# Interleaving the last block's first two accumulations, and moving two of the previous block's stores from SyncE to GpSimd

## The chip, the cores and the metric

The kernel runs on one core of one Trainium2 chip. The metric is the device time of one execution in microseconds, taken as the median of several runs. The kernel before the change has a median of 667.27 us over three runs (666.69 to 668.64). Beside these runs there is one profiled execution with its own time.

## The reference

The input `x` has 8 sequences of 4096 tokens with 192 channels, in float32. The computation has two stages.

```python
# stage 1: causal convolution of 7 taps per channel; 8 heads of 24 channels share their taps
w = exp(weight - max) / (sum + 1e-9)                 # weight: 8 x 7, a softmax over the taps
out[b, s, h, g] = sum_k w[h, k] * x_pad[b, s + k, h, g]   # 6 zero tokens ahead of each sequence
# stage 2: a feed-forward layer over all 32768 tokens
h = x @ w_in                                          # 192 -> 2048
g = 0.5 * h * (1.0 + erf(h / sqrt(2)))                # exact GELU
return g @ w_out                                      # 2048 -> 192, float32
```

## The kernel before

The 32768 tokens are cut into two halves of 16384, and each half into 35 blocks: six of 256 tokens and then 29 of 512 (`WS`, line 33). A block always takes its tokens from both halves at once. The blocks are numbered 0 to 34, so block 34 is the last (`NB - 1`) and block 33 the one ahead of it (`NB - 2`).

For one block the work runs through the engines like this. SyncE (SP) issues the loads of `x`. VectorE (DVE) transposes them and, with some first taps done by ScalarE (ACT), computes the convolution into `xc`. TensorE (PE) multiplies by `w_in` into two PSUM buffers `hp` (line 1292). ACT applies GELU and writes `gT` (line 1199). PE multiplies `gT` by `w_out` into the four PSUM banks `ob`. DVE or ACT copies the result to the buffer `osb` in SBUF (there are two, used in turn), and DMAs store it to the output in HBM.

The second product comes in several forms. Block 33 is one of the blocks (`ST`, line 75) whose second product is built from sums of `gT` blocks, so that fewer products are needed (line 1426). Its four banks must then be combined. ACT copies parts out (`st_copy`, line 782). GpSimd (POOL) issues two small DMAs, `cg` and `cu`, that move 64 partitions to the other 64 (`st_dma`, line 686). DVE adds them (lines 803 and 797) and writes three transposed pieces into `osb` (line 815); these pieces are the events `ev` of the list for stage 35 (line 109). The last of them, `ev.1.33`, ends block 33.

Block 33 is then stored by `store` (line 829): one wait for `S_EV`, followed by four DMAs, `q` = 0 to 3. Each has 32 partitions with 16 runs of 96 floats, which is 512 runs of 384 bytes or 192 KB. Before the change SP issues all four (line 845).

Block 34 has no other block behind it to share PE with. Its second product (line 1482) is done in four groups `g` of 128 tokens. Each group has two accumulations `h`, one for each half of the tokens, each into a PSUM bank of its own and with 16 products (`NF` = 16), one for each 128 rows of `w_out`. Before a group starts, `wait_banks` (line 416) waits until both of its banks are free: groups 0 and 2 use the `ob` banks that block 33 leaves, groups 1 and 3 the `hp` buffers. In group 0, with `h` = 0, every fourth product also waits for the GELU that it needs; the 13th waits for the last GELU of the kernel. When an accumulation is complete it is copied out, for `h` = 0 by DVE (line 449) and for `h` = 1 by ACT (line 451). Each is then stored by one DMA of 96 KB (`store_half`, line 459), issued by SP for `h` = 0 and by ACT itself for `h` = 1.

Nothing reorders this. Each engine works through a list in the order in which the code writes it, and waits for semaphores: `S_GELU`, `S_MM2` (an accumulation is done), `S_EV` (DVE has written a piece), `S_OUT` (a store has landed; one for each `osb` buffer). At the end SP waits until both `S_OUT` counts are full (line 1516). Then all five engines meet at the end of the block of code (the trace gives this line 201): each runs a DRAIN, the other four announce themselves to POOL, and POOL, after its own DRAIN, releases all.

POOL's own list ends with `cg` and `cu` of block 33 (`GLIST`, line 858), so its DRAIN comes right behind these two DMAs.

Of the kernel before, what the change touches and what calls it, by code (L numbers as in the profile page):

```python
# [11 lines left out]
def bass_lightweight_conv__then__act_gelu_exact_kernel(  # L12
# [10 lines left out]
    F2, C = moe_w_out.shape  # L23
# [13 lines left out]
    NB = len(WS)  # L37
# [3 lines left out]
    NF = F // 128  # L41
# [27 lines left out]
    SL0 = [sum(NSL[:n]) for n in range(NB + 1)]  # L69
    NG = [w // 128 for w in WS]  # L70
# [111 lines left out]
    OUTS = []  # L182
# [12 lines left out]
    def sem(name):  # L195
        return es.enter_context(nc.semaphore(name))
# [4 lines left out]
    with es:  # L201
# [37 lines left out]
        S_XIN = [sem("S_XIN%d" % i) for i in range(NX)]  # L239
        S_XP = sem("S_XP")  # L240
        S_OUT = [sem("S_OUT%d" % i) for i in range(2)]
        S_MSET = sem("S_MSET")
        S_WNM = sem("S_WNM")
        S_IDN = sem("S_IDN")
# [581 lines left out]
                    ap(xin[n % NX], 32 * q * (TB // 32 * DQ), dst), ap(xt, off, src)  # L826
                ).then_inc(sm or S_XIN[n % NX], 16)

        def store(e, m):
            if m < M0:  # L830
                for g in range(NG[m]):
                    wait_ev(e, m, g)
                    e.dma_start(
                        ap(
                            outt,
                            (OFF[m] + 128 * g) * C,
                            [[C, 128], [HALF * C, 2], [1, C]],
                        ),
                        ap(osb[m % 2], g * C, [[8 * C, 128], [4 * C, 2], [1, C]]),
                    ).then_inc(S_OUT[m % 2], 16)  # L840
                return
            wait_ev(e, m, NP - 1)
            for q in range(4):

                e.dma_start(
                    ap(
                        outt,
                        ((q // 2) * HALF + OFF[m]) * C + (q % 2) * (C // 2),
                        [[C, 32], [32 * C, WS[m] // 32], [1, C // 2]],
                    ),  # L850
                    ap(
                        osb[m % 2],
                        32 * q * 8 * C,
                        [[8 * C, 32], [C // 2, WS[m] // 32], [1, C // 2]],
                    ),
                ).then_inc(S_OUT[m % 2], 16)

        GLIST = (
# [15 lines left out]
        @block.gpsimd  # L874
        def _(g):
            def win_in(q, hf, sm):
                c0, pat = part(q)
                g.dma_start(  # L878
                    ap(win, 64 * hf * NP * F + c0, pat), ap(wint, c0 + FQ * hf, pat)
                ).then_inc(sm, 16)  # L880

            g.wait_ge(S_MSET, 1)
            for hf in range(2):
                m = idb[64 * hf : 64 * hf + 64, :]
                g.affine_select(
                    out=m,
                    in_=m,
                    compare_op=ALU.is_equal,
                    fill=0.0,
                    base=0,  # L890
                    pattern=[[-1, 64]],
                    channel_multiplier=1,
                ).then_inc(S_IDN)
            g.wait_ge(S_IDN, 2)
            g.memset(wnm[:, :], 0.0).then_inc(S_WNM)
            g.memset(ap(xTb[0], HF, [[NP * XB, 128], [XB, NP], [1, HB]]), 0.0).then_inc(S_HALO)
            for q in range(2):
                for hf in range(2):
                    win_in(q, hf, S_WIN[(hf, 2 + 3 * hf)[q]])
            g.wait_ge(S_PRO, 9)  # L900
            g.tensor_tensor(  # L901
                ap(dg, 3 * 64, [[KS * 64, 128], [64, KS - 3], [1, 64]]),
                ap(idb, 0, [[64, 128], [0, KS - 3], [1, 64]]),
                ap(wcol, 3, [[32, 128], [1, KS - 3], [0, 64]]),
                ALU.mult,
            ).then_inc(S_DG)

            def wout_in(k):
                g0, gs = ((0, 1), (4, 1), (2, 4), (3, 4))[k]
                g.dma_start(  # L910
                    ap(wout, 2 * g0 * C, [[NF * C, 128], [2 * gs * C, 2], [1, 2 * C]]),
                    ap(woutt, 256 * g0 * C, [[2 * C, 128], [256 * gs * C, 2], [1, 2 * C]]),
                ).then_inc(S_WOUT[k], 16)

            def halo(n):

                t, tw = (xTb[PC[n]], XB) if n in PC else (xT[n % 2], XW)
                dst = ap(t, HF, [[NP * tw, 128], [tw, NP], [1, HB]])
                if n >= 4:
                    g.wait_ge(S_CV, cvd(n - 2))  # L920
                if OFF[n] % SEQ == 0:
                    g.memset(dst, 0.0).then_inc(S_HALO)
                    return
                g.wait_ge(S_TR, trd(n - 1))
                src = ap(
                    xT[(n - 1) % 2], HF + WS[n - 1], [[NP * XW, 128], [XW, NP], [1, HB]]
                )
                if n == NR:
                    g.wait_ge(S_UH, 1)
                    src = ap(uu, 32 - HB, [[TB, 128], [32, NP], [1, HB]])  # L930
                g.tensor_copy(dst, src).then_inc(S_HALO)

            win_in(2, 0, S_WIN[3])
            load(g, 2, (0,), S_XP)
            halo(1)
            g.wait_ge(S_HALO, 2)
            dup(g, 0, 1)
            win_in(2, 1, S_WIN[4])
            wout_in(0)
            load(g, 2, (2,), S_XP)  # L940
            g.wait_ge(S_DUPP, 1)
            cast(g, 1, 0)
            cast(g, 1, 1)
            load(g, 2, (1,), S_XP)
            wout_in(1)
            cast(g, 1, 2)
            load(g, 2, (3,), S_XP)
            wout_in(2)
            wout_in(3)
            halo(2)  # L950
            def win_again(k):
                g.wait_ge(S_MM1, SL0[NR - 1] + (4, 8, 14, 16)[k])
                c0 = 2 * FQ * (0, 2, 1, 3)[k]
                for hf in range(2):
                    for p in range(NP):
                        g.dma_start(
                            ap(win, (64 * hf * NP + p) * F + c0, [[NP * F, 64], [1, 2 * FQ]]),
                            ap(wint, RUN * p * F + c0, [[GRP * F, 8], [F, RUN], [1, 2 * FQ]]),
                        ).then_inc(S_WR[k], 16)

            for n in range(3, 10):
                halo(n)
                for k in {NR: (0,), NR + 1: (1, 2, 3)}.get(n, ()):
                    win_again(k)
            for op in GLIST.split():
                name, *q = op.split(".")
                if name == "halo":
                    halo(int(q[0]))
                else:
                    st_dma(g, int(q[1]), name, int(q[0]))  # L970

        @block.vector
        def _(v):
# [238 lines left out]
        def _(t):  # L1212
# [261 lines left out]
            m = NB - 1  # L1474
            for g in range(NG[m]):
                wait_banks(t, m, g)
                for h in range(2):
                    for i in range(NF):
                        if (g, h) == (0, 0) and i % 4 == 0:
                            t.wait_ge(S_GELU, SL0[m] + i + 4)  # L1480
                        c0 = (2 * i * NG[m] + 2 * g + h) * 128
                        ins = t.matmul(  # L1482
                            banks(m, g)[h],
                            gT[m % 2][:, c0 : c0 + 128],
                            wout[:, CH[h][i] * C : (CH[h][i] + 1) * C],
                            start=(i == 0),
                            stop=(i == NF - 1),
                        )
                    ins.then_inc(S_MM2)

        @block.sync
        def _(sp):
            sp.dma_start(wsb[:, :], ap(wt, 0, [[KS, H], [1, KS]])).then_inc(S_WSB, 16)
            load(sp, 0, (0, 1))

            sp.wait_ge(S_PRO, 2)
            load(sp, 1)
            sp.wait_ge(S_WOUT[3], 16)
            load(sp, 3)
            load(sp, 4)  # L1500
            xs = 5
            for n in range(1, NB):
                while xs < min(NB, AHEAD.get(n, n + 5)):
                    load(sp, xs)
                    xs += 1
                if n + 4 == NR:
                    for q in range(4):
                        sp.dma_start(
                            ap(p5s, 32 * q * TB, [[TB, 32], [1, DQ]]),
                            ap(xt, (q // 2 * HALF + OFF[n + 4] - 32) * D + DQ * (q % 2), [[D, 32], [1, DQ]]),  # L1510
                        ).then_inc(S_XH, 16)
                store(sp, n - 1)
            for g in range(NG[NB - 1]):
                store_half(sp, g, 0)
            for s in range(2):
                sp.wait_ge(S_OUT[s], OUTS[NB - 1 if (NB - 1) % 2 == s else NB - 2])


# [26 lines left out]
```

## Time and profile before

| | us |
|---|---|
| median of three runs | 667.27 |
| time of the profiled execution | 665.89 |
| its span, first to last instruction | 664.2 |
| PE busy | 658.3 (99%) |
| DVE busy | 619.1 (93%) |
| ACT busy | 598.3 (90%) |
| POOL busy | 106.7 (16%) |
| granted TensorE clock | 1.000 |
| time from the end of the last store's issue (ACT, 662.12) to the end of the span | 2.0 |

All times inside the execution count from its first instruction. The change touches only the last 15 us, so the table is of little use by itself: what matters is a timeline of the stretch from 649 to 664 us, engine by engine, and the times at which DMAs are issued and land. A row of the timeline has start, duration, engine, line, operation, the tiles, how many instructions it stands for, and in square brackets how long the engine sat idle ahead of it and what released it. An engine's name with a q behind it (SPq, ACTq, POOLq) is its sequencer, which issues DMAs, waits and drains.

### The profile page before, as it was taken

Reading aid. Unit: us, or ns where it says so; the run is one execution under the profiler, and the core shown is the slowest. Engines: PE = TensorE matmul, PEld = TensorE weight load, DVE = VectorE, ACT = ScalarE, POOL = GpSimd, SP = SyncE. Lnnn points to the kernel's source line nnn. Section 1 sums busy time; section 2 is a strip of 40 time slices with the busy share of each in tenths; the row PEclk is TensorE's granted clock in tenths of the full one; section 3 lists DMA queues with packets and bytes.
Section 4 is the critical chain, followed back from the end, with each engine's and each line's share of the span. In section 5 each row is a group of like instructions: output and inputs, shape, how many; then the busy total and the mean of one; then the engine's idle time right before and its main releaser. Section 6 shows DMA issues by size and latency. Waiting matters only on the chain.

```text
span 664.2 us, 27974 instructions
## 1 busy us (share of the span) xinstructions
PE 658.3 (99%) x12792; PEld 505.6 (76%) x12792; DVE 619.1 (93%) x555; ACT 598.3 (90%) x707; POOL 106.7 (16%) x175
## 2 busy tenths in 40 slices
PE   8999999999999999999999999999999999999998
PEld 8999655576778988777878755767777888777887
DVE  6999879999999999999999999999999999999962
ACT  8899999898899899999989998988998988899883
POOL 7000430102010110202120102011212020111110
PEclk9999999999999999999999999999999999999999
DMA  9749493935673691677444348947545855352364
GB/s 156 163 95 181 74 156 82 218 64 116 150 146 80 141 206 25 164 168 150 94 116 114 65 106 207 200 108 168 113 106 120 177 117 126 66 113 49 86 142 112
DMA packets 146438, 83.66 MB, mean 126 GB/s; under 512 B 129936, under 2 KB 138192, under 8 KB 146320
## 3 DMA queue, kind: packets, MB, share of 16 engines
q1 hardware_dynamic: 129328, 49.42, 34.8%
q0 software_dynamic: 15872, 31.86, 23.7%
q8 instruction: 100, 1.64, 1.1%
q10 hardware_dynamic: 1120, 0.59, 0.3%
q14 instruction: 18, 0.15, 0.1%
HBM read 31.51 MB, written 25.17 MB: 85 GB/s over the span
## 4 chain that ended last, share of the span: by engine, by line
PE 96%; DMA 2%; ACT 1%; DVE 0%; issue 0%; POOL 0%; ACTq 0%; DVEq 0%
PE hp L1292 49%; PE ob L1426 25%; PE ob L1377 16%; PE ob L1332 5%; DMA win<-in_moe_w_in_dram 1%; PE hp L1482 1%; PE ob L1482 1%; DMA p5s<-u 1%; ACT gT L1199 0%; DMA wsb<-in_weight_dram 0%; DVE wcol L996 0%; POOL win L381 0%; DVE p5s L803 0%; POOL win L878 0%; POOL dg L901 0%
## 5 line engine op out<-in xcount | busy, mean ns | idle before, releaser
L1199 ACT ACTIVATE gT<-hp 128x1024 bf16<-128x1024 f32 x510 | 513.3, 1022 | 52.4 <-PE hp L1292 44.8
L1292 PE MATMUL hp<-xc,win 64*64 64x512 bf16 (+2 forms) x6036 | 438.6, 366 | 0.6 <-DVE win L381 0.5
L1292 PEld LDWEIGHTS hp<-xc,win 64*64 64x64 bf16 (+1 forms) x6036 | 241.8, 105 | 75.9 <-ACT gT L1199 7.3
L359 DVE SCALAR_TENSOR_TENSOR acc<-xT,wcol,acc 128x1536 f32<-128x1536 f32 (+1 forms) x165 | 282.0, 1709 | 8.3 <-ACT acc L1157 5.4
L1426 PE MATMUL ob<-gT,wot 64*64 64x512 bf16 x1152 | 219.1, 376 | 0.0
L1426 PE MATMUL ob<-gT,wst 64*64 64x512 bf16 (+2 forms) x1152 | 203.4, 323 | 0.5 <-DVE p5s L803 0.5
L1377 PE MATMUL ob<-gT,wot 64*64 64x512 bf16 x1920 | 135.8, 376 | 0.0
L1426 PE MATMUL ob<-s_S,wot 64*64 64x512 bf16 (+2 forms) x864 | 132.7, 305 | 0.0
L1426 PEld LDWEIGHTS ob<-gT,wst 64*64 64x64 bf16 x1152 | 98.8, 107 | 15.8 <-DVE p5s L803 1.3
L1377 PEld LDWEIGHTS ob<-gT,wot 64*64 64x64 bf16 x1920 | 71.0, 107 | 32.6
L1426 PEld LDWEIGHTS ob<-gT,wot 64*64 64x64 bf16 x1152 | 88.9, 107 | 8.6
L1426 PE MATMUL ob<-s_S,wst 64*64 64x512 bf16 x288 | 79.5, 376 | 0.0
L1426 PEld LDWEIGHTS ob<-s_S,wot 64*64 64x64 bf16 x864 | 68.8, 107 | 11.0 <-issue 0.3
L1157 ACT ACTIVATE acc<-xT,wcol 128x512 f32<-128x512 f32 (+1 forms) x93 | 64.6, 702 | 0.0
L1023 DVE STREAM_TRANSPOSE xT<-xin 128x1536 f32<-128x1536 f32 (+2 forms) x39 | 59.6, 1536 | 2.9 <-DMA xin<-in_x_dram 1.7
L691 POOL DMA_DIRECT2D gT<-gT x36 | 32.0, 907 | 186.3 <-DVE s_S L734 186.3
L1426 PE MATMUL ob<-s_Dn,wst 64*64 64x512 bf16 x216 | 61.0, 376 | 0.0
L359 DVE SCALAR_TENSOR_TENSOR xc<-xT,wcol,acc 128x1536 bf16<-128x1536 f32 (+1 forms) x33 | 56.5, 1713 | 0.6
L734 DVE TENSOR_TENSOR s_S<-gT 128x1024 bf16<-128x1024 bf16 (+1 forms) x54 | 45.7, 853 | 1.6 <-ACT gT L1199 1.6
L1332 PE MATMUL ob<-wout,gT 64*128 64x192 bf16 x768 | 42.0, 243 | 0.0
L1332 PEld LDWEIGHTS ob<-wout,gT 64*128 64x128 bf16 x768 | 35.1, 94 | 3.3
L1426 PEld LDWEIGHTS ob<-s_S,wst 64*64 64x64 bf16 x288 | 30.8, 107 | 4.4
(100 smaller groups left out, 423.6 us busy)
## 6 DMA issues: line engine op xcount, KB each, us to landing
out_dram<-osb SPq DMA_DIRECT2D x124, 192.0 KB, 3.4
xin<-in_x_dram SPq DMA_DIRECT2D x116, 192.0 KB, 4.5
gT<-gT POOLq DMA_DIRECT2D x18, 512.0 KB, 4.9
gT<-gT POOLq DMA_DIRECT2D x18, 256.0 KB, 4.6
dn<-gT POOLq DMA_DIRECT2D x6, 512.0 KB, 3.0
dn<-s_S POOLq DMA_DIRECT2D x6, 512.0 KB, 6.2
xin<-in_x_dram SPq DMA_DIRECT2D x18, 96.0 KB, 2.4
win<-in_moe_w_in_dram POOLq DMA_DIRECT2D x24, 64.0 KB, 3.3
```

Of the source, the lines that this page charges most:

```text
L359: return e.scalar_tensor_tensor(dst, src, wk, a, op0=ALU.mult, op1=ALU.add)
L691: e.dma_start(quad(m, 1, 0, k, k1 - k), quad(m, 0, 0, k, k1 - k), accum_op=ALU.add).then_inc(S_AD["S3.%d" % q], 16)
L734: ins = v.tensor_tensor(t("S1"), quad(m, 1, 0, k, n), quad(m, 1, 1, k, n), ALU.add)
L1023: v.transpose(out, src).then_inc(S_TR)
L1157: a.activation(out=acc[n % 2][:, p * TB : p * TB + w], in_=ap(xT[n % 2], p * XW + HX, [[NP * XW, 128], [1, w]]), func=AF.Copy, scale=wcol[ ...
L1199: a.activation(out=ap(gT[n % 2], (i % 2 * NF + i // 2) * TB if n in ST else i * c * 2 * w, dst), in_=ap(ob, 2 * TB, [[4 * TB, 128], *src[1 ...
L1292: ins = t.matmul(hbuf(u, slice(fo, fo + fw), o, w), ap(win, f1, [[NP * F, 64], [2, fw]]), xc[n % NXC][r, p * TB : p * TB + w], start=(p == ...
L1332: ins = t.matmul(bb[sub], gT[m % 2][r, c0 : c0 + 128], wout[r, CH[sub][i] * C : (CH[sub][i] + 1) * C], start=(ph == 0 and k == 0), stop=(p ...
L1377: ins = t.matmul(bank(BK[m][j], slice(64 * h, 64 * h + 64), w), ap(wot, 64 * hf * NF * C + CH[h][i] * C + 64 * j, [[NF * C, 64], [1, 64]]) ...
L1426: ins = t.matmul(bank(BK[m][bk], slice(64 * cg, 64 * cg + 64))[:, c0 : c0 + w], wt_, x, start=(e == mine[0]), stop=(e == mine[-1] or e in ...
L1482: ins = t.matmul(banks(m, g)[h], gT[m % 2][:, c0 : c0 + 128], wout[:, CH[h][i] * C : (CH[h][i] + 1) * C], start=(i == 0), stop=(i == NF - 1),)
```

## The change

Two independent edits, both at the end of the kernel.

- Block 34, group 0: instead of 16 products for `h` = 0 and then 16 for `h` = 1, PE does the first 12 of `h` = 0, the first 12 of `h` = 1, then the last four of `h` = 0 and the last four of `h` = 1. The wait for the last GELU stands ahead of the 13th product of `h` = 0 as before, which is now the 25th product of the group. Each accumulation is announced when its last product is done. Groups 1 to 3 are unchanged, and so is the number of products.
- Block 33: SP issues the stores `q` = 0 and 1; POOL issues `q` = 2 and 3, behind its last DMA `cu`, after its own wait for `S_EV`. These two count on a new semaphore `S_OG`, and SP's last waits are changed to match: 32 less on one `S_OUT`, and a further wait for 32 on `S_OG`.

```diff
+        S_OG = sem("S_OG")
...
-        def store(e, m):
+        def store(e, m, parts=range(4)):
...
-            for q in range(4):
+            for q in parts:
...
-                ).then_inc(S_OUT[m % 2], 16)
+                ).then_inc(S_OG if parts[0] else S_OUT[m % 2], 16)
...
                     st_dma(g, int(q[1]), name, int(q[0]))
+            store(g, NB - 2, (2, 3))
...
-                for h in range(2):
-                    for i in range(NF):
-                        if (g, h) == (0, 0) and i % 4 == 0:
-                            t.wait_ge(S_GELU, SL0[m] + i + 4)
...
-                    ins.then_inc(S_MM2)
+                cut = (0, NF - 4, NF) if g == 0 else (0, NF)
+                for i0, i1 in zip(cut, cut[1:]):
+                    for h in range(2):
+                        for i in range(i0, i1):
+                            if (g, h) == (0, 0) and i % 4 == 0:
+                                t.wait_ge(S_GELU, SL0[m] + i + 4)
...
+                        if i1 == NF:
+                            ins.then_inc(S_MM2)
...
-                store(sp, n - 1)
+                store(sp, n - 1, range(4) if n < NB - 1 else (0, 1))
...
-                sp.wait_ge(S_OUT[s], OUTS[NB - 1 if (NB - 1) % 2 == s else NB - 2])
+                sp.wait_ge(S_OUT[s], OUTS[NB - 1] if (NB - 1) % 2 == s else OUTS[NB - 2] - 32)
+            sp.wait_ge(S_OG, 32)
```

More of the change, by code (lines that the diff above doesn't have):

```diff
@@ L1476, in _ @@
                 wait_banks(t, m, g)
-                for h in range(2):
-                    for i in range(NF):
-                        if (g, h) == (0, 0) and i % 4 == 0:
-                            t.wait_ge(S_GELU, SL0[m] + i + 4)
[L1481 to L1488, printed above, removed]
-                    ins.then_inc(S_MM2)
+                cut = (0, NF - 4, NF) if g == 0 else (0, NF)
[4 more added lines that the diff above has]
+                                t.wait_ge(S_GELU, SL0[m] + i + 4)
+                            c0 = (2 * i * NG[m] + 2 * g + h) * 128
+                            ins = t.matmul(
+                                banks(m, g)[h],
+                                gT[m % 2][:, c0 : c0 + 128],
+                                wout[:, CH[h][i] * C : (CH[h][i] + 1) * C],
+                                start=(i == 0),
+                                stop=(i == NF - 1),
+                            )
+                        if i1 == NF:
+                            ins.then_inc(S_MM2)
         @block.sync
```

## The prediction

> **What bounds the kernel now.** I read the chain of waits first, since it says which work ends last, and only then the timeline of the same stretch. The page's shares (PE 99%, DVE 93%) are averages over 35 blocks; the change touches the last 15 us alone.
>
> ```profile
> 649.61 0.46 PE ob L1426 x7
> ...
> 650.58 1.01 ACT gT L1199
> 651.60 0.05 issue
> 651.64 1.82 PE ob L1482 x20
> 653.47 2.64 PE hp L1482 x32
> 656.11 2.64 PE ob L1482 x32
> 658.75 2.65 PE hp L1482 x32
> 661.40 0.02 issue
> 661.42 0.33 ACT osb L451
> ```
>
> Columns: start, length, what. For once the chain leaves PE: at 650 us it goes to the last GELU on ACT, because the 13th product of block 34 waits for it, and returns to PE at 651.64. From there PE runs without a gap to 661.40. The timeline shows what stands beside it:
>
> ```profile
> 649.97 1.16 PE L1482 MATMUL ob<-wout,gT 128*128 128x192 bf16 x12
> ...
> 650.98 0.52 POOL L686 DMA_DIRECT2D p5s<-u  x1 [15.63 <-ACT u L782]
> ...
> 651.64 1.82 PE L1482 MATMUL ob<-wout,gT 128*128 128x192 bf16 x20 [0.51 <-ACT gT L1199]
> ...
> 652.19 0.52 POOL L686 DMA_DIRECT2D u<-u  x1 [0.69 <-issue]
> ...
> 655.73 0.71 DVE L815 STREAM_TRANSPOSE osb<-wtf 128x512 f32<-128x512 f32 x1
> ...
> 656.47 2.60 SPq L845 DMA_DIRECT2D out_dram<-osb  x4
> ...
> 659.12 2.57 SPq L459 DMA_DIRECT2D out_dram<-osb  x4
> ...
> 661.78 0.34 ACTq L459 DMA_DIRECT2D out_dram<-osb  x1
> ```
>
> Block 33 is complete at 656.44 (DVE's last transpose), and SP then issues eight stores without a break until 661.69. The last store of all is ACT's, issued from 661.78; SP's last wait ends at 663.77, 2.0 us later, and the span ends at 664.16. What ends the kernel is thus the last product, its copy, its store; SP's queue is only 0.1 us behind that.
>
> The third view is the one for line 201, where the engines meet at the end. Columns: engine, operation, count, shortest/median/longest in ns, first and last start.
>
> ```profile
> L201 POOLq DRAIN  x1: 7748/7748/7748, 652.2 to 652.2; - x1
> L201 PEldq DRAIN  x1: 1675/1675/1675, 659.8 to 659.8; - x1
> L201 DVEq DRAIN  x1: 397/397/397, 660.1 to 660.1; - x1
> L201 ACTq DRAIN  x1: 153/153/153, 662.2 to 662.2; - x1
> L201 SPq DRAIN  x1: 7/7/7, 663.9 to 663.9; - x1
> ```
>
> All engines must finish theirs. PE's, DVE's and ACT's end within 0.2 us of their engine's last work. POOL's is another thing: it starts behind the last DMA that POOL issues (652.17) and ends at 659.91, though that DMA was issued by 652.71 and had landed by 654.92 (2.73 us after issue). Today this costs nothing: 659.91 lies 4 us ahead of SP's DRAIN at 663.94. The change gives POOL two later DMAs.
>
> **The change, part by part.** The sum is made against the profiled execution (span 664.16, time 665.89, 1.4 us under the median) and its difference is added to the median, 667.27.
>
> *The products of group 0.* 32 products take 2.64 us, so one takes 0.083. Now PE does 12 from 649.97 (to 650.96), stands until 651.64, and does 20 more (to 653.30). After: 24 products from 649.97 last until 651.95, when the GELU is done (651.60), so the wait costs nothing, and the other 8 end at 652.61. That moves PE's end by -0.68, from 661.40 to 660.72. Both banks are already granted ahead of the first product, so no wait is added here. The first accumulation is done some 0.3 us later than now (652.28 against 651.97); hidden, as DVE gets to its copy only after block 33, at 656.37. The next wait is group 2's for banks of block 33: DVE's line 803 frees them at 654.06, and group 2 would start at 655.26. Groups 1 and 3 wait for GELUs that are done. ACT's last store would be issued from 661.10 instead of 661.78 and would end at 663.09.
>
> *Two stores off SP.* SP's four stores took 0.32, 0.49, 0.80 and 0.87 us to issue; the last two go, 1.7 us. SP's half stores of groups 0 to 2 start that much sooner, and the one for group 3 then waits for DVE's copy, which ends at 660.46 now and 659.78 after. SP's end is then no later than ACT's. This does not move more bytes per time: from 657.5 to 662.5 the DMA engines are near full, as the windows show (last two columns: DMA share, GB/s).
>
> ```profile
> 657.50:658.50 1.00, 1.00 (x15) 1.00 (x13) 0.32 (x1) 0.00 (x0) 0.00 (x0) 1.00 0.97 257
> 658.50:659.50 1.00, 1.00 (x15) 1.00 (x14) 0.00 (x0) 0.33 (x1) 0.00 (x0) 1.00 0.88 202
> 659.50:660.50 1.00, 1.00 (x15) 1.00 (x14) 0.36 (x1) 0.00 (x0) 0.00 (x0) 1.00 1.02 271
> ```
>
> The stretch holds about 5.35 us of full DMA work; begun at 657.2 it ends at 662.6, which still allows the end at 663.09 plus 0.4. So without POOL both edits together are worth -0.7, PE's part.
>
> *Two stores on POOL.* They stand behind `cu`, which ends at 652.71, so they wait for nothing but `S_EV`, and start at 656.5. Behind them on POOL there is only the DRAIN, for which all engines wait. No row has 512 runs issued by POOL. Rows: 64 runs 0.52 to 0.59 us (line 686), 256 runs 0.62 to 0.75 (line 825). At 0.15 more for 192 runs, 512 take 0.9. The distance of two issues is uncertain: between the last two it was 1.21, with 0.69 of "issue", at the other pairs about 0.55 (no idle time). I take the gap, as the nearest row at the end of POOL's list: first store 656.5 to 657.4, second 658.1 to 659.0. Without the gap: 657.4 to 658.3.
>
> *The DRAIN.* One row, with three ways to count it. From its start 7.75 us; from the end of the last issue 659.91 - 652.71 = 7.21; from the last landing 659.91 - 654.92 = 4.99. (7.75 would fit a cost for each DMA: POOL issued 128, 60.5 ns each; the trace does not show whether it is so.) After the change these give: from the start, 658.1 + 7.75 = 665.85; from the issue's end, 659.0 + 7.21 = 666.2; from the landing, with 4.1 us from issue to landing as POOL's loads of `x` have, 662.2 + 4.99 = 667.2. I take the middle one. The other DRAINs end behind their engine's last work, and for POOL that is the issue. From the last DRAIN to the end of the span it is 664.16 - 663.94 = 0.22. So the span ends at 666.4, **+2.3**, and the median becomes 669.5. The low end of this case is the start reading without the gap: 657.4 + 7.75 + 0.22 = 665.4, +1.2, 668.5. The high end is the landing reading with the longest landing that SP's stores show near the end, 4.9: 663.0 + 4.99 + 0.22 = 668.2, +4.0, 671.3. In this case PE's 0.7 us are lost: the end no longer hangs on PE.
>
> One rule speaks for a further delay. DVE's copies of line 449 take 1.03 us between 656.37 and 657.82, beside POOL's issues; but POOL issued in 0.56 us at 634.23 and 0.57 at 634.78 with DVE busy throughout, so I add nothing. The Trainium skill's page "SBUF — State Buffer", section "Who interferes with whom", says that certain DVE modes (a float32 copy within SBUF among them) keep GpSimd from writing descriptors; these copies read PSUM. Were it to hold here, it would add up to 1.0.
>
> **The rivals.**
>
> *POOL's DRAIN does not hold the end.* Its length may belong to what POOL did before, not to its last DMAs: there is one row only, and POOL's first DRAIN, before any DMA, took 0.18 us. It decides if the DRAIN lasts under 5.0 us from 658.1, so that it ends before SP's at 663.3. Then the time is 667.27 - 0.7 = 666.6, faster than before, by about 0.1%. Against it: 7.75 us of DRAIN, 5.0 after all had landed, with nothing else on POOL. The Trainium skill's page "VectorE: DVE Perf Modes", section "The DRAIN you can't avoid", says that the DRAINs of preamble and postamble last some 12 ns on all five engines, which would give this rival; SP's 7 ns agree, POOL's 7748 do not, and the row decides.
>
> *The stores by POOL land last.* SP now waits for them too (`S_OG`). They share full DMA engines with SP's and ACT's stores. POOL's landings reach 8.2 us (line 691, accumulating, 4.8 median): 658.1 + 8.2 + 0.4 = 666.7, +2.5, 669.8. It decides from 5.3 us on, as 658.1 + 5.3 = 663.4. For it: full engines. Against: the stretch's work is done at 662.6.
>
> *The change is hidden on PE.* If ACT, SP or the stores ended the kernel without PE, the 0.7 would be zero: 667.3. For it: SP's queue, 0.1 us behind; but that queue gets shorter by 1.7.
>
> **How the numbers follow.** No change can be told from a change of up to 0.3% here, 2.0 us. The DRAIN holds the end: 0.70, of which 0.47 above 669.3 and 0.23 between 668.5 and 669.3. Hidden DRAIN, with PE's gain or without: 0.22, of which 0.17 within 0.3% and 0.05 for faster by more than that, if the stores also clear sooner than I think. Late landing: 0.08, slower. Together: faster 0.05, same 0.40, slower 0.55. The likeliest case gives 669.5. The range reaches down to the hidden DRAIN, 666.6, and 0.1 less, and up to the landing reading, 671.3, so 666.5 to 671.3. The likeliest case's own range is 668.5 to 671.3.
>
> **What would show it.** PE: one unbroken stretch from 649.97 to 660.7. SP: two stores at line 846 instead of four, then half stores from 657.4. POOL: two issues of about 0.9 us between 656.4 and 659.0, and at line 201 a DRAIN that starts near 658 and ends near 666, behind SP's last wait near 663.2. The forecast is wrong if that DRAIN is short, or follows something else than POOL's last issue; and its size is wrong if POOL's issues stand much closer, or if the DRAIN grows with 512 runs.

## The result, and the profile after

The changed kernel took 670.15 us (median of 13 runs, 668.43 to 670.99) against 667.02 us for the kernel before on the same chip (13 runs, 666.23 to 668.64): a ratio of 1.0048, 95% interval 1.0040 to 1.0057. The medians differ by 3.1 us. Its profiled execution took 668.43 us with a span of 666.70 us, 2.5 us longer than the span of before.

The view of the block's closing line, line 201 again, in the kernel after (engine, operation, count, shortest/median/longest in ns, first and last start):

```profile
L201 POOLq DRAIN  x1: 10195/10195/10195, 656.3 to 656.3; - x1
L201 PEldq DRAIN  x1: 1675/1675/1675, 658.2 to 658.2; - x1
L201 DVEq DRAIN  x1: 397/397/397, 658.5 to 658.5; - x1
L201 ACTq DRAIN  x1: 152/152/152, 660.6 to 660.6; - x1
L201 SPq DRAIN  x1: 7/7/7, 663.1 to 663.1; - x1
```

POOL's DRAIN ends at 656.27 + 10.195 = 666.46. Its row starts 0.10 us ahead of the row of POOL's second store (656.37), which the code issues before it, so the start of the row does not say when the DRAIN can begin. SP, which was the last engine before, is done at 663.06 and then stands for 3.4 us. The span ends 0.23 us behind POOL's DRAIN. The four other lines are what they were, to within 1 ns.

The timeline of the last 18 us (start, length, engine, line, operation, out<-in, count, idle time before and what ended it):

```profile
649.04 2.81 PE L1486 MATMUL ob<-wout,gT 128*128 128x192 bf16 x32
...
651.26 0.52 POOL L687 DMA_DIRECT2D u<-u  x1 [0.69 <-issue]
...
654.61 0.71 DVE L816 STREAM_TRANSPOSE osb<-wtf 128x512 f32<-128x512 f32 x1
...
655.35 0.89 SPq L846 DMA_DIRECT2D out_dram<-osb  x2
...
655.68 1.34 POOL L846 DMA_DIRECT2D out_dram<-osb  x2 [3.90 <-DVE osb L450]
...
656.29 4.08 SPq L460 DMA_DIRECT2D out_dram<-osb  x4
...
656.98 2.80 PE L1486 MATMUL hp<-wout,gT 128*128 128x192 bf16 x32
...
660.18 0.34 ACTq L460 DMA_DIRECT2D out_dram<-osb  x1
```

Group 0 is now one row of 32 products, where before it was 12, a wait of 0.51, and 20. From the first product to the last PE takes 10.74 us instead of 11.42, and ACT's last store is issued at 660.18. So the first half of the change does what it says. SP's four stores of line 845 have become two, and two stand on POOL.

What the views by waits make of the end can mislead. The chain of waits of the kernel after ends with ACT's copy:

```profile
657.14 2.65 PE hp L1486 x32
659.79 0.02 issue
659.82 0.33 ACT osb L452
```

That is 660.15, and 6.5 us of the span lie behind it. SP's own waits name PE (line, what it waited for, total, times, longest):

```profile
SPq L201 <- PEq L201: 3.6, 1, 3.6
```

In the kernel before the same row was 0.2. But PE's DRAIN was over at 659.8. The only thing that ends at 666.46 is POOL's DRAIN, so the row of the closing line, not the name in the wait, tells who was last.

The landing of POOL's two stores, in the view of line 846 on POOL (first line: issue in ns, shortest/median/longest; second: from issue to landing in us):

```profile
L846 POOL DMA_DIRECT2D out_dram<-osb x2: 656/676/696, 655.7 to 656.4; - x2
...
DMA to landing us min/median/max: 4.2/4.7/5.2
```

The second one lands at 661.55, ahead of the last store of all (ACT's, 662.88). From 661.55 to 666.46 it is 4.91 us in which no data of POOL's moves; in the kernel before the same distance was 4.99.

### The profile page after: what moved, and what is told of

It reads as the page before. It is cut to its first block, busy times and chain, and to the rows that moved or that the text cites. A ratio compares the mean times of both kernels' runs of the same rounds, so it can differ in the third digit from the quotient of the medians.

```text
span 666.7 us, 27974 instructions
## 1 busy us (share of the span) xinstructions
PE 657.8 (99%) x12792; PEld 504.5 (76%) x12792; DVE 619.0 (93%) x555; ACT 598.2 (90%) x707; POOL 109.5 (16%) x177
## 4 chain that ended last, share of the span: by engine, by line
PE 97%; DMA 1%; POOL 1%; DVE 0%; issue 0%; ACT 0%; POOLq 0%
PE hp L1294 50%; PE ob L1428 25%; PE ob L1379 16%; PE ob L1334 5%; PE ob L1486 1%; PE hp L1486 1%; DMA win<-in_moe_w_in_dram 1%; POOL win L879 0%; PE ob L1237 0%; POOL xTb L375 0%; DVE win L382 0%; PE ob L1294 0%; DVE xT L1025 0%; POOL idb L886 0%; ACT osb L452 0%
```

## The experiments

The theory after the result: the closing DRAIN of GpSimd waits until the last DMA that GpSimd issued has landed, then works for about 5 us more. Whether these 5 us are fixed or grow with the DMAs issued since its last DRAIN was open at first; the early DRAIN below was to tell. The rivals: the two halves of the change each cost something; the late end comes from the stores' landing; or the 5 us belong to the two stores themselves.

**The products alone.** The kernel before, with the new order of group 0's products and nothing else. SP issues all four stores. Against the kernel before:

```
-                for h in range(2):
-                    for i in range(NF):
...
+                cut = (0, NF - 4, NF) if g == 0 else (0, NF)
+                for i0, i1 in zip(cut, cut[1:]):
+                    for h in range(2):
+                        for i in range(i0, i1):
...
```

> Only the order of block 34's first two accumulations is changed; SP issues all four stores of block 33, as before. The theory (GpSimd's closing DRAIN ends a fixed time, some 4.95 us, behind the landing of GpSimd's last DMA): the DRAIN ends near 659 as before, hidden, and PE's unbroken stretch is worth 0.7 us: median 666.3, ratio 0.999. If instead the product order is what made the changed kernel slower, this run is slower than before: near 670.

Measured: 665.78 us (11 runs, 664.77 to 667.16) against 666.05 on that chip, ratio 0.9998, 0.9989 to 1.0007. Profiled: span 663.03. The timeline and the closing line:

```profile
649.46 2.81 PE L1484 MATMUL ob<-wout,gT 128*128 128x192 bf16 x32
...
655.68 2.43 SPq L845 DMA_DIRECT2D out_dram<-osb  x4
...
658.15 2.94 SPq L459 DMA_DIRECT2D out_dram<-osb  x4
```

```profile
L201 POOLq DRAIN  x1: 7184/7184/7184, 651.7 to 651.7; - x1
L201 SPq DRAIN  x1: 7/7/7, 662.8 to 662.8; - x1
```

From the first product of block 34 to the end of the span it is 663.03 - 649.46 = 13.57 us, against 664.16 - 649.97 = 14.19 before: 0.62 of the 0.68 us arrive at the end, in the trace. The times alone can't show it: the interval holds -0.1% and zero alike. Here POOL's DRAIN is over at 658.86, 4 us ahead of SP's.

**The stores alone.** The kernel after, with the old order of the products; against the kernel after:

```
-                cut = (0, NF - 4, NF) if g == 0 else (0, NF)
-                for i0, i1 in zip(cut, cut[1:]):
...
+                for h in range(2):
+                    for i in range(NF):
...
```

> Only the two stores are moved to GpSimd; the products are in the old order. The theory: the same closing DRAIN as in the changed kernel, ending 4.9 to 5.0 us behind the last landing of the two stores, and the span ends 0.2 us behind it. The product order doesn't matter, since the stores start when DVE has finished block 33: median 670.1, ratio 1.0045 to 1.005. If PE still counted, it would be 0.7 slower than the changed kernel: 670.8.

Measured: 670.42 us (5 runs, 669.59 to 670.95) against 666.05 on that chip, ratio 1.0061, 1.0049 to 1.0073.

```profile
L201 POOLq DRAIN  x1: 10355/10355/10355, 657.8 to 657.8; - x1
L201 SPq DRAIN  x1: 7/7/7, 664.7 to 664.7; - x1
```

The stores alone bring the whole loss: without the products' new order it is at least as large. The ratio is above the 1.0045 to 1.005 that was expected and nearer to what was set for the case that PE still counts (0.7 us more). Its interval overlaps that of the changed kernel, so the times do not decide whether the new order still helps a little while the DRAIN is last. In the trace the DRAIN ends 11.29 us behind block 33's last transpose (668.13 - 656.84), against 11.14 in the changed kernel.

**An early DRAIN.** The kernel after, with a DRAIN put into GpSimd's list ahead of `cg` of block 33, where 126 of its 130 DMAs are behind it and it has idle time. The stores stay on POOL.

```
                 name, *q = op.split(".")
+                if op == "cg.0.33":
+                    g.drain()
```

> The changed kernel, with one more DRAIN on GpSimd ahead of its last two small DMAs (cg and cu of block 33), where it waits 15.6 us anyway. Two readings of the 4.95 us that the closing DRAIN takes behind the last landing. Fixed time: nothing changes at the end, median 670.1, and the closing DRAIN again ends 4.9 to 5.0 us behind the last landing. A cost for each DMA that GpSimd issued since its last DRAIN (4.99 us / 128 = 39 ns before the change, 4.91 / 130 = 38 ns after): the early DRAIN takes 126 of them, some 4.9 us in the idle stretch, the closing one has 4 left and ends 0.2 us behind the last landing, near 662 in the span; then SP's last wait ends the kernel and PE's gain shows: median 666.3, ratio 0.999.

Measured: 666.33 us (12 runs, 665.57 to 668.69) against 666.05, ratio 1.0006, 0.9995 to 1.0016. The rows of the new DRAIN (line 969) and of the closing line:

```profile
L969 POOLq DRAIN  x1: 9209/9209/9209, 634.8 to 634.8; - x1
```

```profile
L201 POOLq DRAIN  x1: 5737/5737/5737, 657.2 to 657.2; - x1
L201 SPq DRAIN  x1: 7/7/7, 664.3 to 664.3; - x1
```

The loss is gone with the stores still on POOL. The closing DRAIN now ends at 662.98, 0.22 us behind the landing of the second store (662.76), where it was 4.91. The early one ends at 644.03, 6.60 us behind the last landing ahead of it (637.43), beside other work. So the 5 us are neither fixed nor the price of these two stores: they are a remainder from the DMAs before, and it can be paid earlier. Had the landing of the stores been the cause of the loss, this kernel would still be some 0.5% slower.

The miss: the 0.999 that was expected did not come. The end is now SP's last wait, and the last store lands later: from the first product of block 34 to the end of the span it is 664.50 - 650.14 = 14.36 us, where the products alone took 13.57. The DMA view from 660.5 to 664.5 us (one digit for each 0.1 us, the busy tenths of the DMA engines; below it the last store, ACT's, with its time to landing), first of the products alone, then of the early DRAIN:

```profile
DMA  9889966988899998300000000000000000000000
...
out_dram<-osb ACTq DMA_DIRECT2D x1, 96.0 KB, 1.8
```

```profile
DMA  6999999797896985689999865443222000000000
...
out_dram<-osb ACTq DMA_DIRECT2D x1, 96.0 KB, 2.8
```

In the first the engines stop together: from 8 tenths to none in some 0.2 us. In the second it takes 0.8 us, a part of the engines still working while the others stand. In the kernel after it is the same (0.7 us, and 2.7 us for ACT's last store); in the kernel before, and with the stores on ACT below, the fall takes 0.2 to 0.3 us, and that store 2.0 and 2.1. Over all traces in which block 33's stores run beside the last ones, ACT's last store takes 2.6 to 2.9 us with POOL's two stores among them (five traces) and 1.8 to 2.1 without (three). The last landing is 0.65 us later behind block 33's last transpose than with the products alone (7.63 against 6.98), which is about PE's 0.7 us. Which engines are late, and why, these views do not tell.

**The same two stores on ACT.** The kernel after, with GpSimd's two stores issued by ScalarE, behind its half store of group 1.

```
-            store(g, NB - 2, (2, 3))
...
+                if g == 1:
+                    store(a, NB - 2, (2, 3))
```

> The changed kernel, but ACT instead of GpSimd issues the two stores, between its second and third copy of block 34. The theory (the DRAIN of GpSimd is the whole loss): hidden DRAIN, as in the run with the products alone; SP's queue is 1.7 us shorter besides, so 666.0 to 666.4. If the loss came from four stores being in flight from two queues at once, or from SP's new wait, it would stay: near 670.

Measured: 665.39 us (11 runs, 664.96 to 666.46) against 666.05, ratio 0.9990, 0.9981 to 0.9998.

```profile
657.32 0.85 SPq L846 DMA_DIRECT2D out_dram<-osb  x2
657.32 0.93 ACTq L846 DMA_DIRECT2D out_dram<-osb  x2
658.21 3.56 SPq L460 DMA_DIRECT2D out_dram<-osb  x4
```

```profile
L201 POOLq DRAIN  x1: 7218/7218/7218, 652.9 to 652.9; - x1
L201 SPq DRAIN  x1: 7/7/7, 664.2 to 664.2; - x1
```

POOL's DRAIN is out of the way again (660.17), the last landing is 6.69 us behind block 33's last transpose (6.98 with the products alone, 7.31 before, 7.56 after, 7.63 with the early DRAIN), and from the first product to the end it is 13.62 us. This is the only version that was measured faster than the kernel before, by 0.1%, 0.7 us: as much as PE's gain. It is not told apart from the products alone, whose interval overlaps it. The Trainium skill's page "DMA: Bandwidth & Descriptors", section "Issuing engines are not separate DMA queues", says that issuing from several engines saves only the issuing engine's time; the 1.0006 with POOL and the early DRAIN and the 0.9990 with ACT agree with that: less time at SP's queue made nothing faster beyond PE's 0.7 us.

**DRAINs at several counts.** The kernel after, with three DRAINs in GpSimd's program: behind 14 DMAs, behind 24 more, behind 44 more. 48 are left for the closing one.

```
+            g.drain()
             for n in range(3, 10):
...
+            g.drain()
             for op in GLIST.split():
...
+                if op == "cu.0.20":
+                    g.drain()
```

> The changed kernel with three more DRAINs on GpSimd, so that the DMAs issued since the last DRAIN number 14 (behind the loads of the start), 24 (behind the second load of w_in), 44 (ahead of the DMA cu of block 20) and, at the closing one, 48. The theory (a DRAIN goes on, behind the last landing, by a cost for each DMA since the last DRAIN; 6.60 us for 126 in the run with one early DRAIN, so 52 ns each): 0.7, 1.3, 2.3 and 2.5 us behind the last landing; the closing DRAIN then ends some 2.4 us sooner than in the changed kernel and is still last by about 1 us: ratio 1.001 to 1.002, between the changed kernel and the run with one early DRAIN. The rival (the long DRAIN belongs to a number of DMAs near 128, a full list, and a short one to any smaller number): all four end within 0.3 us of the last landing, and the ratio is that of the run with one early DRAIN, 1.000. A second rival (a fixed 5 us for any DRAIN behind DMAs that have not landed yet): 5 us each, ratio 1.005.

Measured: 666.90 us (10 runs, 665.76 to 668.56) against 666.21 on that chip, ratio 1.0006, 0.9993 to 1.0019. The four DRAINs, each from its own view:

```profile
L962 POOLq DRAIN  x1: 7003/7003/7003, 12.3 to 12.3; - x1
```

```profile
L967 POOLq DRAIN  x1: 10608/10608/10608, 86.8 to 86.8; - x1
```

```profile
L971 POOLq DRAIN  x1: 5304/5304/5304, 372.5 to 372.5; - x1
```

```profile
L201 POOLq DRAIN  x1: 7381/7381/7381, 657.3 to 657.3; - x1
```

By length they make no sense: 44 DMAs take half of what 24 take. Counted from the last landing, which the trace's records of these DMAs give, they do: 0.63 us for 14, 1.02 for 24, 2.02 for 44, 2.01 for 48. The closing one ends at 664.63, 0.5 us behind SP's; it was expected to be last by about 1. The number of DMAs is what fits, not their size: GpSimd's queue moved 1.97 MB in 2912 packets ahead of the first DRAIN and 1.58 MB in 3456 packets between the first and the second, whose remainder is 1.6 times as long, and 14.42 MB in 4800 packets ahead of the third.

**A DRAIN ahead of the last `cu`.** One thing did not fit: 126 DMAs left 6.60 us in the early DRAIN, 130 left 4.91 in the closing one. In the kernel before and after, the issue of `cu` of block 33 comes 0.69 us late with no wait that the profile shows. It is GpSimd's 128th DMA. If this gap were the clearing of a part of the list, a DRAIN just ahead of it would find the whole list, and the gap would go.

```
+                if op == "cu.0.33":
+                    g.drain()
```

> The changed kernel with one more DRAIN on GpSimd between cg and cu of block 33, behind 127 DMAs, one fewer than the 128 of the kernel before. It holds cu back and so block 33, and the kernel gets slower by several us; only that DRAIN is to be read. Theory (a cost of 42 to 55 ns for each DMA since the last DRAIN; the 128th DMA itself clears part of the list, in the 0.69 us by which it is late in every run without an early DRAIN): 127 DMAs give 5.3 to 7 us behind the last landing, near the 6.60 of 126, and more than the 4.99 of 128; and cu is issued without the 0.69 us. Rival (126 in the earlier run was dear for another reason, the load of that stretch for instance): near 5.0.

Measured: 673.0 us in a single run (666.21 for the kernel before on that chip), as `cu` and all of block 33 wait behind the DRAIN.

```profile
L969 POOLq DRAIN  x1: 9159/9159/9159, 650.5 to 650.5; - x1
```

```profile
660.21 0.52 POOL L687 DMA_DIRECT2D u<-u  x1 [9.12 <-issue]
```

It ends 6.65 us behind the last landing (653.05) for 127 DMAs: 52 ns each, as with 126. `cu` is issued 0.51 us behind the DRAIN's end (659.70), so whether the 0.69 us are gone can't be read here. The closing DRAIN of this run, with 3 DMAs left, ends 0.18 us behind the last landing.

**Only the DRAIN behind 14 DMAs.** Of the three DRAINs above, the first alone. 116 are left for the closing one, so `cu` is the 114th since the last DRAIN, not the 128th.

> The changed kernel with one more DRAIN on GpSimd at its start, behind the first 14 DMAs, which leaves 116 for the closing one. Theory (a cost for each DMA since the last DRAIN, with nothing cleared on the way, as fewer than 128 are listed): 116 x 42 to 52 ns = 4.9 to 6.0 us behind the last landing, which is no better than the 4.91 of the changed kernel though 14 fewer are left; and cu of block 33 is issued 0.5 us behind cg instead of 1.2. The time is that of the changed kernel or up to 1 us more. Rival (any early DRAIN shortens the closing one): clearly under 4.9.

Measured: 669.06 us in a single run, against 666.21.

```profile
L201 POOLq DRAIN  x1: 10238/10238/10238, 656.9 to 656.9; - x1
```

```profile
651.84 0.52 POOL L687 DMA_DIRECT2D u<-u  x1 [0.69 <-issue]
```

The gap stayed, against what was expected, so it does not take 128 DMAs since the last DRAIN. The remainder is 4.79 us, with the gap, for 116, a little under the 4.9 to 6.0 that was expected. It is open what the gap is. Of the kernels here it was there wherever 116 or more were listed at the end (before, after, the first two experiments, the stores on ACT, this one) and not in those with the early DRAIN or the three, where `cu` followed at 0.51 us; and only with it is the remainder 5 us or less for more than 100 DMAs. In these rows the remainder does not grow with the count (4.99 to 5.00 us for 128, 4.91 for 130): taken alone they would fit a fixed 5 us as well, and the growth is shown by the other rows.

All DRAINs of GpSimd that follow DMAs, side by side (us; worked out from start and length in the rows above and the landing records of its DMAs):

| DRAIN | DMAs since the last DRAIN | length | last landing | end | end behind landing | ns per DMA |
|---|---|---|---|---|---|---|
| ahead of `cu`, closing | 3 | 5.39 | 670.07 | 670.24 | 0.18 | 59 |
| early DRAIN, closing | 4 | 5.74 | 662.76 | 662.98 | 0.22 | 55 |
| three DRAINs, first | 14 | 7.00 | 18.72 | 19.35 | 0.63 | 45 |
| 14 drained, first | 14 | 6.77 | 18.54 | 19.16 | 0.63 | 45 |
| three DRAINs, second | 24 | 10.61 | 96.36 | 97.38 | 1.02 | 43 |
| three DRAINs, third | 44 | 5.30 | 375.77 | 377.79 | 2.02 | 46 |
| three DRAINs, closing | 48 | 7.38 | 662.62 | 664.63 | 2.01 | 42 |
| early DRAIN, early | 126 | 9.21 | 637.43 | 644.03 | 6.60 | 52 |
| ahead of `cu` | 127 | 9.16 | 653.05 | 659.70 | 6.65 | 52 |
| 14 drained, closing (gap) | 116 | 10.24 | 662.31 | 667.10 | 4.79 | 41 |
| before, closing (gap) | 128 | 7.75 | 654.92 | 659.91 | 4.99 | 39 |
| products alone, closing (gap) | 128 | 7.18 | 653.87 | 658.86 | 5.00 | 39 |
| stores on ACT, closing (gap) | 128 | 7.22 | 655.17 | 660.17 | 5.00 | 39 |
| after, closing (gap) | 130 | 10.20 | 661.55 | 666.46 | 4.91 | 38 |
| stores alone, closing (gap) | 130 | 10.36 | 663.22 | 668.13 | 4.91 | 38 |

The length goes from 5.3 to 10.6 with no order; the last columns have one. In the rows without the gap it is 42 to 59 ns for each DMA, behind the last landing (the 59 is 0.18 us divided by 3).

## Why the prediction was right, and where its sizes were off

It forecast 669.5 us, slower, by POOL's closing DRAIN; measured were 670.15. The DRAIN was the cause: take the DRAIN's remainder away (the early DRAIN) or move the stores to another engine (ACT), and the loss is gone.

- *The products of group 0: -0.68 at PE, and lost to the end.* Right, to the digit: 11.42 to 10.74 us, one unbroken stretch. The products alone bring 0.62 of it to the end in the trace, so the rival of a change hidden on PE was not what held it back there. With the DRAIN last, the end hangs on block 33's stores and not on PE; the times of the stores alone (1.0061, against 1.0048 with the new order) leave room for a part of it.
- *Two stores off SP.* SP's half stores began 656.29 - 655.32 = 0.97 us after the last transpose of block 33, predicted 0.96. The queue's saving is much smaller than 1.7 us in the end, as its half stores then took 0.54, 0.97, 1.10 and 1.34 us to issue: SP's last issue ended 5.04 us behind that transpose, against 5.25 before. It did not matter.
- *Two stores on POOL.* They were taken to start at the release, to cost 0.9 us each and to stand 0.69 apart. They started 0.36 after the release, cost 0.70 and 0.66, and stood back to back: 512 runs cost no more than the 0.62 to 0.75 of 256. The last issue ended 1.70 us behind the release, not the 2.6 that the prediction had. The gap came ahead of `cu` and not ahead of the last DMA of the list.
- *No delay by DVE's copies.* Right: three copies of line 450 run beside these issues, which were shorter than expected. The Trainium skill's page "SBUF — State Buffer" (section "Who interferes with whom") says that DVE copies in certain modes block GpSimd. The prediction did not count these copies, which read PSUM, among them, and the delay of up to 1.0 us that it set beside that rule is not in these rows; no run here has a copy within SBUF at this place.
- *The DRAIN.* This is the term that was mis-sized. Of three readings the prediction took the one from the end of the last issue (7.21 us). That distance is 6.64 in the trace of the products alone (652.22 to 658.86) and 9.44 in the kernel after (657.02 to 666.46), so it is no constant. The distance from the last landing is nearly one, 4.91 to 5.00 in five traces. The prediction had named it as a sign of being wrong that the DRAIN follows something else than POOL's last issue; by that sign this step was wrong, and the reading that it set aside for its high end, from the landing, was the one that held. Counted from the release, the prediction had the DRAIN's end 9.8 us later by the reading that it took (656.4 to 666.2), and 10.8 by the landing; measured it is 11.14 (655.32 to 666.46), of which 6.23 to the landing and 4.91 behind it. The issue's end came 0.9 us sooner than predicted and the distance behind it was 2.2 to 2.4 us longer: two errors of opposite sign, which left the forecast of +2.3 us within 1 us of the measured +3.1. That the number came so near is in part luck. The span of the profiled execution is nearer still, +2.5 us, but only because block 33 was ready 1.1 us sooner there (655.32) than in the trace of the kernel before (656.44). The landing itself took 5.2 us, not the 4.1 that POOL's loads had shown. The prediction also read the DRAIN of the kernel before as starting behind POOL's last issue (652.17); the row of that issue starts at 652.19, so the row's start does not stand behind it.
- *The remark that 7.75 us would fit a cost per DMA* was near the truth in kind and wrong in size: 42 to 59 ns behind the landing where there was no gap, and 39 in the very row that it was made from, not 60.5 from the start.
- *The rival of a hidden DRAIN, 666.6.* It didn't occur, but it was made to occur by the early DRAIN, and the price was wrong: not -0.7 us but +0.4 us (+0.06%, -0.05 to +0.16%). It left out the slow tail of the transfers that POOL's stores bring. Its argument from the Trainium skill's page "VectorE: DVE Perf Modes" (section "The DRAIN you can't avoid", some 12 ns for the DRAINs at the program's end on all engines) falls with the rows: 7 ns on SP, but 10195 ns on POOL.
- *The rival of a late landing.* POOL's stores landed at 661.55, ahead of SP's last (662.24) and ACT's (662.88): it did not hold the end. The 5.2 us were 0.1 us short of the point that the prediction named; with the stores alone and with the early DRAIN it was 5.3, and ACT's store still landed later.

## What to carry to other kernels

In this kernel, a DMA that GpSimd issues near the end brings GpSimd's closing DRAIN with it: its remainder starts when that DMA has landed, and it is the longer the more DMAs GpSimd has issued since its last DRAIN (0.2 us for 3 or 4, 2.0 for 44 to 48, 4.8 to 6.6 for 116 to 130). Look at the rows of the closing line by engine, not at the chain of waits alone, before you move work to an engine that is idle at the end; where the store must stay there, a DRAIN in an idle stretch earlier pays the list beside other work. An engine with 16% busy time is not free: what it still has to clear counts, and here ACT, at 90%, was the better place for the same two stores (0.9990 against 1.0048).

## What the runs showed of the hardware

- GpSimd's DRAIN ended behind the landing of its DMAs every time, by 42 to 59 ns per DMA issued since the last DRAIN (nine DRAINs without the gap, 3 to 127 DMAs). Bytes and packets of these DMAs do not fit it. The other engines' closing DRAINs do not vary so: PE 1675, ACT 152 or 153, SP 7 ns in all traces, DVE 397 ns in all but the one with the DRAIN ahead of `cu`.
- At the 128th DMA of GpSimd's program an issue came 0.69 us late, in six of the nine traces, and the remainder at the end was then 4.8 to 5.0 us instead of the 6.6 of 126 and 127 DMAs. What that is stays open.
- GpSimd moved its stores of 192 KB in packets of 4224 and 3840 bytes, 11 and 10 runs of 384 bytes, where SP's stores moved as packets of 384; its first data came 2.5 us after issue against 0.9, its stores landed 4.2 and 5.2 us after issue, and the DMA engines then stopped over 0.7 to 0.8 us instead of 0.2 to 0.3.
- The clock granted to TensorE had no part in it: 0.997 over the span, with 0.91 and 0.50 only in the last 5.2 us, when PE had ended.
